# A gated recurrence and a four-branch merge: second layers taken two blocks at a time in the order H, L, D, w1 reloads two beats later, attention inputs and w2 asked for earlier

One Trainium2 chip, one core. The metric is the device time of one execution in microseconds (us), the median of several runs; less is better.

## The reference

```python
# attention: a recurrence per (batch, head), 4 x 8 x 768 x 48
for t in range(S):
    state = alpha[:, :, t, :, None] * state + np.einsum('bhd,bhe->bhde', k[:, :, t], v[:, :, t])
    y[:, :, t] = np.einsum('bhd,bhde->bhe', q[:, :, t], state)
# x = y as (3072, 384); then four branches, w1[e] 384 x 1024, w2[e] 1024 x 384
p = domain_probs / (domain_probs.sum(-1, keepdims=True) + 1e-09)
for e in range(E):
    h = np.maximum(x @ w1[e], 0.0)
    out += p[:, e:e + 1] * (h @ w2[e])
```

## The kernel before

The 24 blocks of 128 rows are worked in seven groups of 2, 4, 4, 4, 4, 4 and 2. For each group and branch, `up` computes the hidden layer in eight chunks of 128 features and `down` the second layer for each block. The attention of the next group runs in small steps between these matmuls (`advance`).

A number is split in three parts: `top` (H below), `low` (L) and `dif` (D). In the profile of before a block's split second layer takes 24 matmuls of 0.174 us, 4.2 us, a raw one 5.3 us; that it takes three parts to be exact enough is the kernel's premise. A product then takes three matmuls: L and H parts are summed in one PSUM tile, D parts in another. The first two groups still use raw weights in places, split them and store the split tiles in a "kept" copy in HBM; later groups load the copy. The four middle groups use split weights in both layers: 16 second layers of 4 x 24 matmuls.

```python
    def split_piece(l, i):                       # a raw w1 or w2 tile becomes a split one
        ...                                      # ACT, yield, ACT, yield, then
        nc.vector.scalar_tensor_tensor(out=low, ...)
        nc.vector.tensor_sub(dif, low.bitcast(F32), top.bitcast(F32))
        nc.gpsimd.dma_start(out=kept[l][i % (E * NQ)], in_=w.bitcast(F32))
        if l == 0 and i + NQ < E * NQ:
            del wt[0][i]
            load_piece(0, i + NQ)                # raw w1 of the next branch, on the sync queue

    def hidden_parts(x, parts):                  # end of a chunk of up
        top, low, dif = parts
        nc.scalar.activation(out=top, in_=x, func=ACT.Relu, scale=TRIM)      # H
        yield
        nc.vector.scalar_tensor_tensor(out=low, in0=x, ...)                  # L
        make_dif(*(part[:, :n // 2] for part in parts))                      # D, first two blocks
        later.append([part[:, n // 2:] for part in parts])                   # D, others, in down

    def down(gi, e, slot):                       # one block
        ...
        sums = [ps.tile([P, DM], F32, name=f"ops{j}", tag="g", bufs=4) for j in range(2 ...)]
        kinds = (1, 0), (2,)                     # (L, H) for each chunk, then D for each chunk
        for n, (kind, fc) in enumerate(...):
            ...
            for part in kind:
                nc.tensor.matmul(sums[part // 2], lhsT=h[:, part], rhs=w[:, part], ...)
        ...                                      # acc += p * sum, on the DVE, for both sums
```

In the profile of the kernel before, L567 is this last matmul, L520 makes H, L522 L and L530 D; L497 adds the two sums of the first layer; L480 and L488 are matmuls of `up`; L203 and L204 ask for raw w1, L206 for raw w2, L160 for alpha, k and q, L222 stores a kept tile; L580 adds a sum to the output. The changed kernel has the same lines under other numbers, given where they are shown.

In the views, PE is TensorE (PEld its weight loads, PEclk its granted clock in tenths), DVE is VectorE, ACT ScalarE, POOL GpSimd, and SPq the sync engine's DMA queue. A line of a waits view gives who waited, for what, and then the us in total, the number of waits and the longest. A line of a timeline gives start and duration in us, and in brackets the idle time before it and what ended that.

## Time and profile before

| | before |
|---|---|
| median of 4 runs | 1132.24 us (1131.76 to 1134.52) |
| span of the profiled run | 1132.4 us |
| TensorE busy | 1076.6 us |
| half-clock time of TensorE | 27 us in six stretches |
| DMA | 273.68 MB, mean 242 GB/s |

TensorE is the bound (busy for 1076.6 of 1132.4 us); what can be won is its idle time and the stretches in which its clock is at half. The prediction below shows the lines that tell who causes the idle time.

### The profile page before, as it was taken

The numbers are of one execution on the slowest core, as the hardware profiler recorded it, in microseconds if no ns is written. First come the engines' busy times: TensorE is split into PE (matmuls) and PEld (weight loads), VectorE is DVE, ScalarE is ACT, GpSimd is POOL, SyncE is SP. The second block draws the span as 40 slices with busy tenths as digits, with TensorE's granted clock in tenths as the row PEclk, the third lists the DMA queues.
The fourth block names the chain that finished last, engine by engine and source line by source line (L and its number), as shares of the span: only waits on it lengthen the run. The fifth ranks groups of instructions, "written<-read, shape, count | busy, mean of one in ns | idle before, by whom it ended". The sixth has DMA issues, their size and how long they took to land.

```text
span 1132.4 us, 21704 instructions
## 1 busy us (share of the span) xinstructions
PE 1076.6 (95%) x8532; PEld 896.4 (79%) x8532; DVE 751.5 (66%) x1625; ACT 561.2 (50%) x1191; POOL 35.5 (3%) x75
## 2 busy tenths in 40 slices
PE   8968898899999999999999999999999999999898
PEld 8746675676767798888898988898988888888676
DVE  4557776466566878777987776987776867656111
ACT  5747665565557545435546435555445344322221
POOL 2000000000000100000000000000000000000000
PEclk9989999999999999999999999999999999999999
DMA  8376869786777968548668559567569557743882
GB/s 122 108 253 190 276 212 330 282 278 241 282 236 239 364 215 337 228 149 342 217 195 339 202 178 346 183 232 304 205 210 347 203 207 290 308 183 160 296 304 74
DMA packets 166197, 273.68 MB, mean 242 GB/s; under 512 B 120624, under 2 KB 140976, under 8 KB 142032
## 3 DMA queue, kind: packets, MB, share of 16 engines
q1 hardware_dynamic: 156704, 230.06, 59.0%
q0 software_dynamic: 6016, 42.08, 9.3%
q8 instruction: 67, 1.10, 0.4%
q10 hardware_dynamic: 3376, 0.17, 0.3%
q14 instruction: 34, 0.28, 0.1%
HBM read 229.81 MB, written 42.47 MB: 240 GB/s over the span
## 4 chain that ended last, share of the span: by engine, by line
PE 72%; DVE 12%; ACT 7%; DMA 4%; issue 3%; SPq 2%; ACTq 0%; DVEq 0%
PE ops L567 21%; PE one L488 16%; PE ops L565 13%; PE two L488 7%; PE sc L324 4%; PE yps L411 4%; DVE hT L522 3%; DVE t L497 3%; PE one L480 3%; PE tp L259 3%; ACT hT L520 2%; ACT qb L298 2%; DMA ra<-in_alpha_dram 2%; DVE near L334 2%; DMA hT<-in_moe_w_dram 2%
## 5 line engine op out<-in xcount | busy, mean ns | idle before, releaser
L567 PE MATMUL ops<-w,hT 128*128 128x384 f32 x1536 | 289.3, 342 | 15.6 <-DVE hT L522 15.3
L567 PEld LDWEIGHTS ops<-w,hT 128*128 128x128 f32 x1536 | 266.7, 189 | 23.5 <-DVE hT L522 20.1
L488 PE MATMUL one<-xT,w 128*128 128x512 f32 (+1 forms) x1104 | 275.4, 385 | 0.1
L488 PEld LDWEIGHTS one<-xT,w 128*128 128x128 f32 x1104 | 194.7, 188 | 42.8 <-issue 3.2
L565 PE MATMUL ops<-hT 128*128 128x384 f32 x512 | 181.0, 500 | 10.3 <-DMA hT<-in_moe_w_dram 10.3
L495 ACT ACTIVATE t<-one 128x512 f32<-128x512 f32 (+1 forms) x184 | 102.9, 559 | 147.1 <-PE one L488 146.5
L298 ACT COPY qb<-QT 64x256 f32<-64x256 f32 x336 | 136.5, 406 | 67.9 <-DVE QT L279 38.5
L565 PEld LDWEIGHTS ops<-hT 128*128 128x128 f32 x512 | 94.9, 194 | 69.3 <-DMA hT<-in_moe_w_dram 7.5
L488 PE MATMUL two<-xT,w 128*128 128x512 f32 (+1 forms) x552 | 148.5, 377 | 0.0
L520 ACT ACTIVATE hT<-t 128x512 fp32r<-128x512 f32 x128 | 80.9, 632 | 99.9 <-DVE t L497 98.7
L522 DVE SCALAR_TENSOR_TENSOR hT<-t,hT 128x512 fp32r<-128x512 f32 x128 | 88.7, 693 | 61.2 <-ACT hT L520 59.8
L488 PEld LDWEIGHTS two<-xT,w 128*128 128x128 f32 x552 | 100.3, 188 | 19.8
L580 DVE SCALAR_TENSOR_TENSOR acc<-ops,p_all,acc 128x384 f32<-128x384 f32 x88 | 54.3, 617 | 83.9 <-PE ops L565 48.6
L530 DVE SCALAR_TENSOR_TENSOR hT<-hT 128x256 fp32r<-128x256 f32 x256 | 101.6, 423 | 4.4
L497 DVE TENSOR_TENSOR t<-t,two 128x512 f32<-128x512 f32 x128 | 87.3, 682 | 20.1 <-PE two L488 12.0
L334 DVE COPY_PREDICATED near<-masks,sc 128x256 f32<-128x256 uint8 x144 | 77.0, 535 | 25.0 <-PE sc L324 22.2
L305 DVE TENSOR_TENSOR QT<-QT,dec 128x256 f32<-128x256 f32 x144 | 60.7, 422 | 43.1 <-ACT qb L298 42.6
L324 PEld LDWEIGHTS sc<-qb,KT 128*64 128x64 f32 x2304 | 72.5, 138 | 9.4 <-issue 6.9
L500 DVE TENSOR_TENSOR hT<-t,two 128x512 f32<-128x512 f32 (+1 forms) x56 | 32.1, 574 | 70.6 <-ACT t L495 61.9
L324 PE MATMUL sc<-qb,KT 128*64 128x64 f32 x2304 | 76.7, 223 | 0.3 <-ACT qb L298 0.3
L317 DVE TENSOR_TENSOR KT<-KT,dec 128x256 f32<-128x256 f32 x144 | 60.4, 420 | 3.3 <-PE tp L259 3.3
L316 ACT COPY KT<-KT 128x256 f32<-128x256 f32 x144 | 59.7, 415 | 3.1
(79 smaller groups left out, 936.5 us busy)
## 6 DMA issues: line engine op xcount, KB each, us to landing
w<-kept SPq DMA_DIRECT2D x156, 1152.0 KB
kept<-w POOLq DMA_DIRECT2D x32, 1152.0 KB, 7.3
hT<-in_moe_w_dram SPq DMA_DIRECT2D x48, 384.0 KB
w<-in_moe_w_dram SPq DMA_DIRECT2D x60, 128.0 KB
ra<-in_alpha_dram SPq DMA_DIRECT2D x23, 192.0 KB
rk<-in_k_dram SPq DMA_DIRECT2D x23, 192.0 KB
rq<-in_q_dram SPq DMA_DIRECT2D x23, 192.0 KB
out_dram<-acc POOLq DMA_DIRECT2D x22, 192.0 KB, 2.9
```

Of the source, the lines that this page charges most:

```text
L298: nc.scalar.copy(out=qb[rows, :, i, :].rearrange("p a (b r) -> p a b r", r=m), in_=qv[rows])
L305: nc.vector.tensor_mul(qv, qv, spread(dv[:, :, :, 0], m))
L324: nc.tensor.matmul(out[HALF * s:HALF * (s + 1), 2 * p:2 * p + 2, :], lhsT=KTs[li][:, p, HALF * s:HALF * (s + 1)], rhs=qbs[li][:, p, :, QUA ...
L334: nc.vector.copy_predicated(near.rearrange("p a (b two r) -> p a b two r", two=2, r=m)[:, :, :, 1, :], mk.unsqueeze(1).broadcast_to([P, H, ...
L488: nc.tensor.matmul(out, lhsT=w[:, part, kc], rhs=xTs[gi][:, part, kc, :n], start=(part == terms[0] and kc == 0), stop=(part == terms[-1] a ...
L495: nc.scalar.activation(out=t, in_=one, func=ACT.Copy, scale=FINE)
L497: nc.vector.tensor_add(t, t, two)
L520: nc.scalar.activation(out=top, in_=x, func=ACT.Relu, scale=TRIM)
L522: nc.vector.scalar_tensor_tensor(out=low, in0=x, scalar=0.0, in1=top.bitcast(F32), op0=ALU.max, op1=ALU.subtract)
L530: nc.vector.scalar_tensor_tensor(out=dif, in0=top.bitcast(F32), scalar=1 / 4096.0, in1=low.bitcast(F32), op0=ALU.mult, op1=ALU.subtract)
L565: nc.tensor.matmul(sums[0], lhsT=h[:, 2].bitcast(F32), rhs=w, **ends)
L567: nc.tensor.matmul(sums[part // 2], lhsT=h[:, part], rhs=w[:, part], start=(fc == 0 and part != 0), stop=(fc == FCH - 1 and part != 1))
```

## The change

Its intent: fewer stalls of TensorE. (1) `down` takes two blocks of a split layer at a time, first all H products of both, then all L, then all D, so that L and D of the last chunk are wanted later. (2) alpha, k and q of a next block are asked for as soon as each buffer has been read. (3) The reload of a raw w1 tile waits two more beats of the background work, so that it doesn't stand ahead of those inputs in the sync queue. (4) Raw w2 is asked for earlier in the second and the last group. (5) The splits of the next x are spread over the last branch. (The new `down` also makes the D parts and takes the attention and background steps at other matmuls; with (3), up to four tiles may be split at once, not three.)

```diff
@@ split_piece, background
         if l == 0 and i + NQ < E * NQ:
+            for _ in range(2):
+                yield
             del wt[0][i]
             load_piece(0, i + NQ)
-        if making and len(splitting) < 3:
+        if making and len(splitting) < 4:
@@ attention
         nc.scalar.copy(out=AT, in_=turned(pair(ra)))
+        after = u + 2 if u == 0 else u + 1 if u > 1 else len(units)
+        load(after, "a")
         ...
+        load(after, "k")
         ...
         nc.vector.tensor_mul(QT, turned(pair(rq)), AT)
-        load(u + 2 if u == 0 else u + 1 if u > 1 else len(units), "akq")
+        load(after, "q")
@@ up
-        if fc in ((0,) if gi == 0 else (2, 4)) and begins and not split2(gi, e):
-            half = range(NQ) if gi == 0 else range(fc - 2, fc)
+        if fc in ((0, 2) if gi == 1 else (0,)) and begins and not split2(gi, e):
+            half = range(fc, fc + 2) if gi == 1 else range(NQ)
@@ down (cut)
-    def down(gi, e, slot):
+    def down(gi, e, slots, between):
+        sums = [[ps.tile([P, DM], F32, name=f"ops{j}", tag="g", bufs=4)
+                 for j in range(2 if halves_ else 1)] for _ in slots]
+        steps = [(part, i, fc) for part in ((0, 1, 2) if halves_ else (3,))
+                 for i in range(len(slots)) for fc in range(FCH)]
+        for n, (part, i, fc) in enumerate(steps):
             ...
+            if part >= 2 and fc == FCH - 1:
+                add_up(gi, e, slots[i], sums[i])
```

More of the change, by code (lines that the diff above doesn't have):

```diff
@@ L535, in rectified @@
         yield
-    def down(gi, e, slot):
-        cb, b = groups[gi][slot]
+    def down(gi, e, slots, between):
         first = (gi * E + e) * NQ
-        if slot == 0 and makes[1](gi, e):
+        halves_ = split2(gi, e)
+        if slots[0] == 0 and makes[1](gi, e):
             making.extend(split_piece(1, first + k) for k in range(NQ))
-        if makes[0](gi, e) and 0 < e < E - 1 and slot == 0:
+        if slots[0] == 0 and makes[0](gi, e) and 0 < e < E - 1:
             making.extend(split_piece(0, first + k) for k in range(2, NQ))
-        cols = slice(slot * P, (slot + 1) * P)
-        sums = [ps.tile([P, DM], F32, name=f"ops{j}", tag="g", bufs=4)
-                for j in range(2 if split2(gi, e) else 1)]
-        kinds = (1, 0), (2,)
-        for n, (kind, fc) in enumerate((kind, fc) for kind in (kinds if split2(gi, e) else ((),))
-                                       for fc in range(FCH)):
-            c, f = divmod(fc, FPQ)
-            h = hidden[c][:, :, f, cols]
-            ends = dict(start=(fc == 0), stop=(fc == FCH - 1))
-            if split2(gi, e):
-                w = wt[1][first + c].rearrange("p t (c d) -> p t c d", d=DM)[:, :, f]
+        sums = [[ps.tile([P, DM], F32, name=f"ops{j}", tag="g", bufs=4)
[3 more added lines that the diff above has]
+        for n, (part, i, fc) in enumerate(steps):
+            c, f = divmod(fc, FPQ)
+            h = hidden[c][:, :, f, slots[i] * P:(slots[i] + 1) * P]
+            advance(cost(1, gi, e) / FCH / (3 if halves_ else 1))
+            while between and n >= between[0][0] * len(steps):
+                between.popleft()[1]()
+            if n == len(steps) // 2:
+                background()
+            if later and n % 5 == 4:
+                make_dif(*later.popleft())
+            if halves_:
+                w = wt[1][first + c].rearrange("p t (c d) -> p t c d", d=DM)[:, part, f]
+                nc.tensor.matmul(sums[i][part // 2], lhsT=h[:, part], rhs=w,
+                                 start=(fc == 0 and part != 1), stop=(fc == FCH - 1 and part != 0))
@@ L556, in down @@
             else:
                 w = wt[1][first + c].rearrange("p (c d) -> p c d", d=DM)[:, f]
-            if n:
-                advance(cost(1, gi, e) / FCH * (len(kind) / 3 if split2(gi, e) else 1))
-            if n == FCH // 2:
-                background()
-            if later and n % 4 == 3:
-                make_dif(*later.popleft())
-            if not kind:
-                nc.tensor.matmul(sums[0], lhsT=h[:, 2].bitcast(F32), rhs=w, **ends)
-            for part in kind:
-                nc.tensor.matmul(sums[part // 2], lhsT=h[:, part], rhs=w[:, part],
-                                 start=(fc == 0 and part != 0), stop=(fc == FCH - 1 and part != 1))
@@ L569, in down @@
-        while later and slot == len(groups[gi]) // 2 - 1:
-            make_dif(*later.popleft())
+                nc.tensor.matmul(sums[i][0], lhsT=h[:, 2].bitcast(F32), rhs=w,
+                                 start=(fc == 0), stop=(fc == FCH - 1))
+            if part >= 2 and fc == FCH - 1:
+                add_up(gi, e, slots[i], sums[i])
+        background()
+        if slots[-1] == len(groups[gi]) - 1:
+            while makes[1](gi, e) and (making or splitting):
+                background()
+            for c in range(NQ):
+                del wt[1][first + c]
+                if c < NQ // 2:
+                    load_piece(1, first + NQ + c)
+                else:
+                    late.append(first + NQ + c)
@@ L571, in down, with add_up @@
+    def add_up(gi, e, slot, sums):
+        cb, b = groups[gi][slot]
         at = b * NCB + cb
@@ L586, in down @@
                 out=out[row:row + P, :], in_=acc))
-        background()
-        while slot == len(groups[gi]) - 1 and makes[1](gi, e) and (making or splitting):
-            background()
-        if slot == len(groups[gi]) - 1:
-            for c in range(NQ):
-                del wt[1][first + c]
-                if c < NQ // 2:
-                    load_piece(1, first + NQ + c)
-                else:
-                    late.append(first + NQ + c)
     def cost(layer, gi, e):
@@ L684 @@
             advance(cost(0, 0, 0) / 2)
-        down(0, 0, 0)
+        down(0, 0, [0], deque())
         while waiting:
@@ L696 @@
                 advance(cost(0, gi, e) / (2 if rest else 1))
-            if e == E - 1 and gi + 1 < len(groups):
-                behind = {0: [0], 1: [1, 2]} if len(groups[gi]) == 2 else {1: [0], 2: [1], 3: [2]}
-            else:
-                behind = {}
-            for slot in range(rest, len(groups[gi])):
-                if slot in behind:
-                    split_x(gi + 1, behind[slot])
-                down(gi, e, slot)
-                advance(cost(1, gi, e) / FCH * (2 / 3 if split2(gi, e) else 1))
+            each = 2 if split2(gi, e) else 1
+            turns = [range(k, k + each) for k in range(rest, len(groups[gi]), each)]
+            for k, slots in enumerate(turns):
+                between = deque()
+                if e == E - 1 and gi + 1 < len(groups):
+                    for kc in range(KC):
+                        at = (kc + 1) / (KC + 1) * len(turns) - k
+                        if 0 <= at < 1:
+                            between.append((at, lambda kc=kc: split_x(gi + 1, [kc])))
+                down(gi, e, slots, between)
                 if gi == len(groups) - 1 and e == E - 1:
```

## The prediction

> **What bounds the kernel now.** I read the page's first two parts first (who is busy, slice by slice), then TensorE's own waits, then the timeline around the longest of them.
>
> ```profile
> PE 1076.6 (95%) x8532; PEld 896.4 (79%) x8532; DVE 751.5 (66%) x1625; ACT 561.2 (50%) x1191; POOL 35.5 (3%) x75
> PEclk9989999999999999999999999999999999999999
> ```
>
> TensorE is busy for 1076.6 of 1132.4 us. The change removes no matmul, so all it can touch is the other 56 us and the few slices where the clock is not full. Who causes the idle time is told by the view of TensorE's waits:
>
> ```profile
> PE ops L567 <- DVE hT L522: 15.3, 13, 1.8
> PE ops L565 <- DMA hT<-in_moe_w_dram: 10.3, 5, 3.4
> PE tp L259 <- DMA ra<-in_alpha_dram: 9.9, 2, 9.7
> PE yps L411 <- ACT lat L396: 6.6, 5, 2.9
> PE far L379 <- ACT qb L298: 4.3, 5, 1.3
> PE one L480 <- DMA w<-in_moe_w_dram: 1.7, 1, 1.7
> ```
>
> L567 is the second layer of the four middle groups (split weights, 16 layers of 96 matmuls), L565 that of the outer groups (raw weights). The change aims at the first three lines: 35.5 us. The first is thirteen small stalls, one at the start of nearly every split second layer; the third is one stall of 9.7 us. The timeline of the sync engine's queue shows the cause of that one, and TensorE's timeline what it costs:
>
> ```profile
> 57.88 6.96 SPq L203 DMA_DIRECT2D w<-in_moe_w_dram  x2
> 64.89 2.56 SPq L204 DMA_DIRECT2D w<-in_moe_w_dram  x1
> 67.55 1.31 SPq L160 DMA_DIRECT2D ra<-in_alpha_dram  x1
> ...
> 75.07 1.09 PE L259 MATMUL tp<-ident,ra 128*128 128x128 f32 x4 [9.71 <-DMA ra<-in_alpha_dram]
> 75.95 2.77 PE L480 MATMUL one<-xT,w 128*128 128x256 f32 x6
> ```
>
> The next block's alpha is asked for at 67.55 only, because a raw w1 reload ahead of it sits in the same queue from 57.88 to 67.45. TensorE wants alpha at 65.4.
>
> The timeline of the start of one split second layer, all engines:
>
> ```profile
> 951.33 2.59 PE L567 MATMUL ops<-w,hT 128*128 128x384 f32 x14
> 951.84 0.58 ACT L495 ACTIVATE t<-one 128x512 f32<-128x512 f32 x1
> 951.96 0.69 DVE L522 SCALAR_TENSOR_TENSOR hT<-t,hT 128x512 fp32r<-128x512 f32 x1 [0.70 <-ACT hT L520]
> 952.69 0.42 DVE L530 SCALAR_TENSOR_TENSOR hT<-hT 128x256 fp32r<-128x256 f32 x1
> 953.03 0.68 DVE L497 TENSOR_TENSOR t<-t,two 128x512 f32<-128x512 f32 x1
> 953.75 0.63 ACT L520 ACTIVATE hT<-t 128x512 fp32r<-128x512 f32 x1 [1.33 <-DVE t L497]
> 954.41 0.69 DVE L522 SCALAR_TENSOR_TENSOR hT<-t,hT 128x512 fp32r<-128x512 f32 x1 [0.70 <-ACT hT L520]
> 955.16 2.01 PE L567 MATMUL ops<-w,hT 128*128 128x384 f32 x10 [1.23 <-DVE hT L522]
> ```
>
> TensorE runs 14 matmuls (L and H of hidden chunks 0 to 6, in pairs) at 0.174 us each and stops at the L part of chunk 7. That chunk's H is ready at 954.38 (end of L520), its L at 955.10 (end of the last L522).
>
> [...]
> - [...] nothing of L567 starts between matmul 14's want and 955.16.
> - [...] six L480 matmuls took 2.77 us after the 9.7 us stall and 1.46 us elsewhere, and the granted clock of 70 to 75 us was 0.50.
> - [...]
>
> **The change, part by part.**
>
> (1) Order H, L, D over two blocks. It removes no work. It moves the first use of chunk 7: before, its L at matmul 14; after, its H at matmul 7, as H of the first block runs through all eight chunks before the second block begins. In the layer shown: matmul 7 is reached at 951.33 + 7 x 0.174 = 952.55, H is there at 954.38, so a stall of 1.9 us. It then reaches matmul 14 at 954.43 + 7 x 0.174 = 955.65, where before it was 955.16: 0.5 us later, not sooner. Nothing in the diff shortens the chain that makes H of chunk 7 (copy 0.58, the DVE's L and half D of chunk 6 at 0.69 and 0.42, add 0.68, H 0.63). I read the same four times in all 16 layers: the stall after the change (H of chunk 7, less when matmul 7 is reached) is 1.5 to 3.0 us in twelve, 0.2 to 0.7 in four, sum 26 us. Before, the same layers lost 17 us (the view says 15.3, as it counts a matmul's modelled tail as busy). **About +9.5 us.**
>
> (2) All four PSUM tiles in one pair. Before, a block's two sums had 24 matmuls (4.2 us and more) until a later block needed their banks. After, the next pair's first matmul needs the first block's sum only eight matmuls (1.4 us) after that block's last. The DVE adds take 0.62 us each. I measured, for each block, how long after its last matmul starts the add of its first sum ends: in nine of 16 layers the second block's is under about 1 us, so no stall; in five it is 1.4 to 2.4; in the last layers of two groups (near 532 and 704 us), where the DVE has the next x to split, it is 4.9 us. With both blocks' adds together at the end, the first block's first sum comes some 1.35 us before the second's. In those two layers that leaves a stall of 2.5 us each; in the five about 0.4. **About +7 us.**
>
> (3) Attention inputs asked for once used, w1 reloads two beats later. The 9.7 us stall can go: alpha is asked for near 51 us, where the DMA engines are nearly idle (share 0.22 from 50 to 55 us), and the reload no longer stands ahead of it. But from 55 to 65 us they are at 0.94, mostly with the kept-weight stores, and the same bytes have still to come. In the kernel before, the third and fourth raw w1 tiles of the next layer are asked for at 74.2 and 76.3 and are just in time only because TensorE has lost 9.7 us. Without that loss it wants them about 69 and 73 us, and the last now stands behind the raw w2. So I take 4 of the 9.7 back as a new wait for raw w1, about 4 us. Less half-clock time afterwards (2.77 to 1.46 and smaller ones) is within this. **About -6 us**, between -1 and -12.
>
> (4) Raw w2 asked for earlier. In the second group at the first and third instead of third and fifth chunk: 3.0 us of stall at 211 us goes, with 1 us of half clock (0.69 granted from 210 to 215). In the last group all at once: 1.6 and 2.0 us at 1056 and 1061 us go, with 1 us of clock. The 3.4 us stall at 176 us is in the first group, whose request isn't moved. **About -8.5 us**, if the DMA engines, at 0.95 to 1.05 there, deliver w2 first.
>
> (5) Next x spread: the same three splits at the same places for the four-block groups. **0.**
>
> Sum: +9.5 + 7 - 6 - 8.5 = +2 us on 1132.
>
> **Rivals.**
> (A) The early stretch is cured fully and the order costs little: if TensorE's stall in (1) gives the DVE time to catch up, the adds of (2) come in time. Then +9.5 - 12 - 10 = -12: 1120. For it: the DVE is idle in the stall. Against: in the two worst layers the DVE timeline has no gap over 0.1 us from 536 to 555 us.
> (B) The intent holds: H first means that TensorE waits for less, and the 15.3 us go as well: about 1105. For it: in layers where H of chunk 7 is early (1.5 us after the start in two of them) nearly nothing is lost. Against: in twelve of 16 it is later than 2.9 us.
> (C) The wait only changes name early on: raw w1 or w2 land as late as alpha did, gain (3) is nothing, and (2) is worse, 12 us: 1145. For it: DMA at 0.94; against: the idle DMA before 55 us is now used.
>
> **Range and chances.** The sum is 1134; since the person who made the order chose it for some reason that I may not see, I shade it towards (A) and say **1131 us**. Extremes of (A) and (C) with a little more give 1116 to 1145. Faster by over 2% needs under 1109.5, which only (B) gives: 0.05. Slower by over 2% needs 1154.8, beyond (C): 0.03. Within 2%: 0.92.
>
> **What would show it right or wrong.** Right: the waits of L567 name ACT's H part (L520's successor) instead of DVE's L, over 20 us in all, and some for the DVE's adds near 543 and 715 us; the 9.7 us wait for alpha is gone with a few us for raw w1 between 60 and 80 us; no wait for w2 at 211 and 1056 us. Wrong: L567's waits for H under 12 us (then (1) fails), no waits for adds (then (2) fails), or the first 110 us shortened by 10 us or by nothing (then (3) is mis-sized).

Where the prediction says banks, it means the PSUM tiles of the code's rotation (`bufs=4`).

## The result

| | before | after |
|---|---|---|
| median of 4 runs | 1132.24 us | 1147.02 us (1145.63 to 1147.94) |
| ratio, 95% interval | | 1.0125 (1.0108 to 1.0143) |
| span of the profiled run | 1132.4 us | 1146.2 us |
| half-clock time of TensorE | 27 us | 38 us |

A ratio is the mean time of one kernel's fast runs over that of the other's fast runs of the same rounds, so it is not quite the ratio of the medians. The change made the kernel 1.25% slower: within 2%, as predicted, but 2 us beyond the predicted range and on the side that the sum of the steps pointed to.

The first two parts of the page of the changed kernel, and its TensorE waits:

```profile
PE 1080.6 (94%) x8532; PEld 900.0 (79%) x8532; DVE 752.4 (66%) x1625; ACT 562.7 (49%) x1191; POOL 35.5 (3%) x75
PEclk9989898999999999999999999999999999999999
```

```profile
PE one L485 <- DMA w<-in_moe_w_dram: 23.6, 10, 9.1
PE ops L568 <- ACT hT L525: 23.2, 15, 2.1
PE yps L416 <- ACT lat L401: 4.9, 4, 3.5
PE ops L568 <- DVE acc L599: 3.6, 2, 1.9
```

(Here L485 is the raw first layer, L568 the split second layer, L525 makes H and L599 adds a sum.) All three waits that the change aimed at are gone: none for L, for alpha or for raw w2. Three others are there in their place: for H instead of L (23.2 against 15.3), for the adds (3.6), and for raw w1 (23.6, where it was 1.7).

Lining up the starts of the same layers in both traces gives a ledger of where the changed kernel falls behind:

| stretch | lag gained by the changed kernel | predicted |
|---|---|---|
| start to the first split second layer (402.5 us of before) | +5.1 us | -10 |
| 402.5 to 1045.9 us (middle groups) | +14.2 us | +16.5 |
| 1045.9 us to the end | -5.6 us | -4.5 |

So the middle and the end came within 2.3 us of what was predicted, and the early stretch did not. Inside it the lag is +14.4 us when the fourth branch's second layer begins (171.3 us of before), after which the missing w2 waits win most of it back. By the waits of that stretch in both traces, raw w1 costs 21.9 us more, alpha 9.9 less, raw w2 6.7 less and the attention steps 3.4 less; 6.8 us more at half clock cost up to 3.4: +5.3 in all.

The timeline of the changed kernel at the start of the same layer that the prediction showed (there at 951.33, here at 969.66; L500 is the copy, L527 makes L, L502 the add; lines of other work are left out):

```profile
969.66 1.38 PE L568 MATMUL ops<-w,hT 128*128 128x384 f32 x7
970.17 0.58 ACT L500 ACTIVATE t<-one 128x512 f32<-128x512 f32 x1
970.30 0.69 DVE L527 SCALAR_TENSOR_TENSOR hT<-t,hT 128x512 fp32r<-128x512 f32 x1 [0.70 <-ACT hT L525]
971.36 0.68 DVE L502 TENSOR_TENSOR t<-t,two 128x512 f32<-128x512 f32 x1
972.08 0.63 ACT L525 ACTIVATE hT<-t 128x512 fp32r<-128x512 f32 x1 [1.33 <-DVE t L502]
972.76 2.00 PE L568 MATMUL ops<-w,hT 128*128 128x384 f32 x10 [1.71 <-ACT hT L525]
```

Seven matmuls, then a stop until H of the last chunk is there: 3.10 us after the start. Before, it was fourteen, and a stop until L was there, 3.83 us after the start. The chain on ACT and DVE takes the same time in both (2.54 us from the start of the copy to the end of H).

The sync queue around the longest new stall. First the last raw w1 tile of the fourth branch in the kernel before (columns: start, duration; the tile ahead of it was asked for at 151.9), then raw w2 and the last two raw w1 tiles in the changed kernel, with what TensorE made of it:

```profile
156.45 1.33 SPq L203 DMA_DIRECT2D w<-in_moe_w_dram  x2
157.83 0.60 SPq L204 DMA_DIRECT2D w<-in_moe_w_dram  x1
```

```profile
160.40 3.37 SPq L206 DMA_DIRECT2D hT<-in_moe_w_dram  x4
163.87 1.38 SPq L203 DMA_DIRECT2D w<-in_moe_w_dram  x2
165.31 0.78 SPq L204 DMA_DIRECT2D w<-in_moe_w_dram  x1
166.19 9.29 SPq L203 DMA_DIRECT2D w<-in_moe_w_dram  x2
175.53 2.02 SPq L204 DMA_DIRECT2D w<-in_moe_w_dram  x1
...
178.02 1.22 PE L485 MATMUL one<-xT,w 128*128 128x256 f32 x2 [9.13 <-DMA w<-in_moe_w_dram]
```

Before, both tiles were asked for ahead of raw w2 (which followed at 158.5). Now they stand behind it, and issuing the last takes from 166.2 to 177.6 us: the kept stores of this branch have begun at 160, and the DMA share of 170 to 175 us is 1.02.

The second longest is in the second branch, where the 9.7 us stall for alpha had been:

```profile
62.33 0.70 PE L485 MATMUL one<-xT,w 128*128 128x256 f32 x2 [1.67 <-DMA w<-in_moe_w_dram]
69.27 2.07 PE L485 MATMUL one<-xT,w 128*128 128x256 f32 x4 [6.24 <-DMA w<-in_moe_w_dram]
```

This is the branch's first raw w1 tile. It was asked for at 51.4 us before, and at 54.8 here, behind alpha and k; the DMA share of the next ten microseconds is 1.05 and 1.01.

### The profile page after: what moved, and what is told of

Same layout as the page of the kernel before. It is cut to its first block, busy times and chain, and to the rows that moved or that the text cites. A ratio compares the mean times of both kernels' runs of the same rounds, so it can differ in the third digit from the quotient of the medians.

```text
span 1146.2 us, 21704 instructions
## 1 busy us (share of the span) xinstructions
PE 1080.6 (94%) x8532; PEld 900.0 (79%) x8532; DVE 752.4 (66%) x1625; ACT 562.7 (49%) x1191; POOL 35.5 (3%) x75
## 4 chain that ended last, share of the span: by engine, by line
PE 75%; DVE 12%; ACT 6%; DMA 4%; issue 2%; SPq 1%; POOL 0%; DVEq 0%; ACTq 0%; POOLq 0%
PE ops L568 22%; PE one L493 16%; PE ops L572 13%; PE two L493 7%; PE sc L329 4%; PE yps L416 4%; DMA w<-in_moe_w_dram 4%; DVE t L502 3%; DVE hT L527 3%; PE tp L261 3%; PE one L485 3%; ACT hT L525 3%; DVE near L339 2%; ACT qb L303 1%; PE sps L437 1%
## 5 line engine op out<-in xcount | busy, mean ns | idle before, releaser
L568 PE MATMUL ops<-w,hT 128*128 128x384 f32 x1536 | 293.8, 345 | 26.9 <-ACT hT L525 23.2
L568 PEld LDWEIGHTS ops<-w,hT 128*128 128x128 f32 x1536 | 269.9, 191 | 35.7 <-ACT hT L525 28.5
L493 PEld LDWEIGHTS one<-xT,w 128*128 128x128 f32 x1104 | 195.0, 188 | 41.4 <-issue 3.2
L500 ACT ACTIVATE t<-one 128x512 f32<-128x512 f32 (+1 forms) x184 | 103.1, 560 | 164.2 <-PE one L493 163.7
L572 PE MATMUL ops<-hT 128*128 128x384 f32 x512 | 176.2, 491 | 0.0
L527 DVE SCALAR_TENSOR_TENSOR hT<-t,hT 128x512 fp32r<-128x512 f32 x128 | 88.7, 693 | 61.0 <-ACT hT L525 59.6
L525 ACT ACTIVATE hT<-t 128x512 fp32r<-128x512 f32 x128 | 80.9, 632 | 97.1 <-DVE t L502 95.9
L599 DVE SCALAR_TENSOR_TENSOR acc<-ops,p_all,acc 128x384 f32<-128x384 f32 x88 | 54.3, 617 | 93.2 <-PE ops L572 43.4
L502 DVE TENSOR_TENSOR t<-t,two 128x512 f32<-128x512 f32 x128 | 87.3, 682 | 20.8 <-PE two L493 12.7
L485 PE MATMUL one<-xT,w 128*128 128x256 f32 (+1 forms) x240 | 55.1, 371 | 24.4 <-DMA w<-in_moe_w_dram 23.6
L485 PEld LDWEIGHTS one<-xT,w 128*128 128x128 f32 x240 | 39.6, 205 | 35.3 <-DMA w<-in_moe_w_dram 30.4
```

Of the source, the lines that this page charges most:

```text
L485: nc.tensor.matmul(one, lhsT=w[:, kc], rhs=xraws[gi][:, kc, lo:hi], start=(kc == 0), stop=(kc == KC - 1))
L493: nc.tensor.matmul(out, lhsT=w[:, part, kc], rhs=xTs[gi][:, part, kc, :n], start=(part == terms[0] and kc == 0), stop=(part == terms[-1] a ...
L500: nc.scalar.activation(out=t, in_=one, func=ACT.Copy, scale=FINE)
L502: nc.vector.tensor_add(t, t, two)
L527: nc.vector.scalar_tensor_tensor(out=low, in0=x, scalar=0.0, in1=top.bitcast(F32), op0=ALU.max, op1=ALU.subtract)
L568: nc.tensor.matmul(sums[i][part // 2], lhsT=h[:, part], rhs=w, start=(fc == 0 and part != 1), stop=(fc == FCH - 1 and part != 0))
```

## The experiments

Twelve kernels. "L" below stands for the later reload (with the limit of four tiles that comes with it), "A" for the inputs asked for once used, "W" for the earlier w2, "O" for the new second layer with the spread of x; so the changed kernel is before + L + A + W + O. Runs of one call share the runs of the kernel before, whose median moved between 1129.4 and 1132.9 us from call to call; ratios are the safer figures.

| run | what it is | median us | ratio to before (95%) |
|---|---|---|---|
| m_late | A W O | 1140.14 | 1.0084 (1.0053 to 1.0116) |
| p_late | L | 1131.73 | 1.0010 (0.9980 to 1.0041) |
| m_order | L A W | 1127.77 | 0.9977 (0.9951 to 1.0003) |
| p_order | O | 1149.20 | 1.0181 (1.0143 to 1.0220) |
| p_w2 | W | 1122.01 | 0.9936 (0.9918 to 0.9953) |
| p_attn | A | 1127.38 | 0.9980 (0.9956 to 1.0004) |
| q7 | last chunk last, one block | 1117.79 | 0.9895 (0.9875 to 0.9915) |
| o7 | O with last chunk last | 1131.95 | 1.0020 (0.9993 to 1.0047) |
| q7_w | q7 + W | 1111.21 | 0.9804 (0.9772 to 0.9836) |
| q7_aw | q7 + A W | 1107.77 | 0.9779 (0.9752 to 0.9805) |
| q7_law | q7 + L A W | 1115.45 | 0.9845 (0.9819 to 0.9872) |
| thin | changed kernel, stores a third | 1130.49 (1 run) | not compared |

### The order, undone and alone

m_order is the changed kernel with the old `down`; p_order is the kernel before with the new one. The edits are the last hunk of the diff, taken out or put in alone.

> The changed kernel with the old second layer (one block at a time, L and H in pairs, then D), all else kept. Theory T2 (the order costs what the ledger between 402 and 1046 us shows): 1131 to 1135 us, waits for H gone, waits for L of 14 to 16 us back, no wait for the adds. Rival: the middle lost its 14 us to something else (input requests moved in the queue, weights later), then over 1141 us.

> The kernel before with the new second layer alone (two blocks at a time, H, L, D, with the spread of next x that comes with it). T2: 1144 to 1148 us, with 22 to 25 us of waits for H and 3 to 5 us for the adds. Rival: as the early stretch is untouched, a time within 4 us of before if the middle's loss came from the input requests.

TensorE's waits in p_order:

```profile
PE ops L563 <- ACT hT L520: 23.2, 15, 2.1
PE ops L563 <- DVE acc L594: 3.7, 2, 1.9
```

m_order's longest waits:

```profile
PE one L485 <- DMA w<-in_moe_w_dram: 19.9, 11, 5.5
PE ops L572 <- DVE hT L527: 15.2, 13, 1.8
```

p_order is 1.8% slower than before, and its trace loses 14.2 us in the middle stretch, as the changed kernel does; m_order loses nothing there (it gains 2) and runs at 1127.8, slightly under its expected 1131 to 1135. p_order's 1149.2 is 1 us over its expected range. Both show the waits that were expected. **The order costs the middle groups some 14 us; this holds alone and with the rest.** By the ratios the order costs more, 1.8% alone and 1.5% with the rest (20 and 17 us); what lies beyond the middle has no cause shown. (The traces of before and p_order differ by 13.3 us only, but that of before is one of its slow executions, 1134.2 us, and that of p_order its fastest.) That it isn't the moved input requests is shown by p_order, which has none of them. m_order shows one thing more, for the early stretch: without the new order the waits for raw w1 are still 19.9 us, and by 402.5 us of before it has won 0.5 us and not the 10 predicted.

### When the last chunk is wanted

If the cause is only when chunk 7 of the hidden layer is wanted, then any order that wants it later must win. q7 changes the old `down` for the first block of a layer only:

```diff
+        steps = [(kind, fc) for kind in kinds for fc in range(FCH)]
+        if split2(gi, e) and slot == 0:
+            steps = [s for s in steps if s[1] < FCH - 1] + [s for s in steps if s[1] == FCH - 1]
```

o7 does the like within the two-block order, in a layer's first pair: L and H of chunk 7 of both blocks come after L and H of the other seven. All else is as in p_order, so the two differ by the order alone.

> The kernel before with one change of mine: in the first block of a split second layer, the three products of the last hidden chunk come after all others (L and H of chunks 0 to 6, then D of 0 to 6, then chunk 7), so chunk 7 is wanted at the 22nd matmul (3.7 us after the start) and not at the 15th (2.4 us). Theory (the start of the layer waits for the chain that makes chunk 7, and it is only a matter of when it is wanted): waits for L fall from 15.3 to under 4 us, time 11 to 15 us under before. Rival: TensorE then waits for the D parts or the adds, as the DVE is behind; time within 5 us of before.

> The kernel before with the new second layer (two blocks, H, L, D), but in its first pair H and L of the last hidden chunk of both blocks come after H and L of chunks 0 to 6 (wanted at the 29th matmul). Theory: the 23.2 us of waits for H go to under 3 us, so 18 to 23 us under the run with the new second layer alone, 1126 to 1131 us; the waits for the adds stay at 3 us or grow to 10, as TensorE comes sooner to the end of the pair while the DVE doesn't. Rival: the two-block order costs for another reason, then over 1140 us.

TensorE's waits in the split second layer, q7 first, then o7:

```profile
PE ops L569 <- DVE hT L522: 2.4, 5, 0.6
PE ops L569 <- DVE hT L530: 1.0, 2, 0.5
```

```profile
PE ops L567 <- DVE acc L598: 10.7, 6, 3.8
PE ops L567 <- ACT hT L520: 0.7, 1, 0.7
```

q7 brings the waits for L from 15.3 to 2.4 us and the time down by 1.05%, some 12 us. o7 brings the waits for H from 23.2 to 0.7 us: the two-block order loses them for the same reason. But o7 is no faster than before and 1 us over its expected range, as **the waits for the adds then grow from 3.7 to 10.7 us** (my bound was 10). TensorE comes earlier to the end of a pair, while the DVE doesn't, and both blocks' sums fill all four PSUM tiles. In the kernel before, with one block at a time, the view of TensorE's waits has no wait for the adds. So the two-block order has two costs: it wants H of the last chunk too early, and it leaves no spare PSUM tile (read from the code and these waits; no run had more tiles). The first hides a part of the second.

### The early stretch: one part at a time

> The kernel before with the earlier requests for raw w2 alone. Theory: the waits for raw w2 fall from 10.3 us to under 4 us (the one at 176 us is in the first group and stays), time 6 to 9 us under before. Rival: with the DMA engines at their limit there, w2 comes earlier at the cost of the first layer's weights, then waits for w1 or kept weights grow as much and the time is within 2 us of before.

p_w2 is 0.64% faster (7.2 us by the ratio), within what was expected, and loses no time elsewhere: the raw w2 waits fall from 10.3 to 3.3 us, those for raw w1 stay at 1.8 (1.7 before).

> The kernel before with attention inputs asked for once used, alone (reloads as before). Theory T (the alpha wait is mostly passed on to raw w1, because alpha, k, q and the reloads of this stretch share DMA engines that the kept-weight stores fill from 55 to 68 us): alpha plus w1 waits between 9 and 15 us where before had 11.6, time within 3 us of before. Rival: queue order alone made the alpha wait; then alpha plus w1 waits under 5 us and the time 7 to 11 us under before.

```profile
PE one L483 <- DMA w<-in_moe_w_dram: 5.9, 4, 4.1
PE ops L568 <- DMA hT<-in_moe_w_dram: 5.2, 6, 1.9
...
PE tp L259 <- DMA ra<-in_alpha_dram: 3.2, 1, 3.2
```

In p_attn alpha plus w1 come to 9.1 us (11.6 before), the low end of theory T, and the gain of 0.2% is not clear of noise. Of the 6.7 us that the alpha wait lost, 4.2 came back as waits for raw w1, even with the reloads at their old place.

### The later reload

m_late is the changed kernel with the two extra beats and the limit of four taken out; p_late is before with them put in.

> The changed kernel with the later w1 reloads taken out (no two extra beats, at most three tiles in the making), all else of the change kept. Theory T (the later reload, behind raw w2 and attention inputs in the sync queue, makes the 23.6 us of waits for raw w1): those waits fall under 8 us, the alpha wait of 9.7 us stays away or is under 4 us, and the time is 1128 to 1137 us. Rival R (the DMA engines are full, so the alpha wait was passed on to w1 and would be with any order of the queue): waits for w1 and alpha together stay over 15 us and the time is 1142 to 1147 us.

> The kernel before with the later w1 reloads alone. T: waits for raw w1 appear (8 to 20 us), as the last two tiles of each layer still come behind raw w2; the alpha wait shrinks, as the reload no longer stands ahead of it; time 1132 to 1145 us. R: the sum of the alpha and w1 waits stays near the 11.6 us of before, time 1130 to 1135 us.

The waits of m_late up to 200 us:

```profile
PE one L483 <- DMA w<-in_moe_w_dram: 10.9, 3, 4.6
...
PE tp L259 <- DMA ra<-in_alpha_dram: 3.5, 1, 3.5
```

Neither side of the expectation was met by m_late: w1 plus alpha wait 14.4 us (T said w1 under 8, R said the sum over 15), and the time, 1140.1, lies between. The later reload thus makes some 9 of the 23.6 us, not all. What it costs the changed kernel in time is not shown by this pair: 1.0125 and 1.0084, and their intervals overlap. In p_late the w1 waits come to 15.4 us and alpha's shrink to 1.8; a sum of 17.2 against 11.6, as T said. Yet p_late costs nothing clear in time (1131.7, within R's range and just under T's): by 334 us its layers lag by 0.6 us, and its waits for raw w2 are 4.1 us in all against 10.3 before. A later pair shows the cost plainly: q7_law against q7_aw, which differ by the later reload alone.

> The same with the later w1 reloads too, so the whole change but its order of the second layer, with mine in its place. If the later reload costs by itself: 3 to 7 us over the run without it (1108 to 1116 us), with waits for raw w1 of 15 to 22 us. Rival: the later reload is harmless without the two-block order: within 2 us of the run without it.

```profile
PE one L485 <- DMA w<-in_moe_w_dram: 20.8, 9, 6.1
```

> The same with attention inputs asked for once used (reloads as before). If that adds its own -2 to -7 us: 1103 to 1110 us. Rival: the alpha wait passed on to w1, 1110 to 1114 us.

```profile
PE one L483 <- DMA w<-in_moe_w_dram: 6.2, 3, 4.2
...
PE tp L259 <- DMA ra<-in_alpha_dram: 3.6, 1, 3.6
```

With it 1115.45, without it 1107.77 us on the same chip: 7.7 us, a little over the 3 to 7 expected. The rival, that it is harmless without the two-block order, falls for this setting; p_late, without A and W, showed no cost.

### Why the wait is passed on: the kept stores

The remaining question is whether the queue's order makes these waits or the DMA engines are full. thin leaves the order of the queue as in the changed kernel and takes away two thirds of the bytes stored for w1:

```diff
-        nc.gpsimd.dma_start(out=kept[l][i % (E * NQ)], in_=w.bitcast(F32))
+        nc.gpsimd.dma_start(out=kept[0][i % (E * NQ)][:, 0], in_=w[:, 0].bitcast(F32))   # l == 0
```

> The changed kernel, but of each split w1 tile only the first third is stored to the kept copy (and read back three times), so the result is wrong on purpose and only the stretch up to 185 us is judged: the stores there are 0.38 MB instead of 1.15 MB each, the order of the queue is the same. Theory T (the early waits are the DMA engines filled by the kept stores, whatever the order): the waits for raw w1 up to 185 us fall from 23.6 to under 8 us. Rival Q (the order of the sync queue alone: w1 behind inputs and raw w2): they stay over 15 us.

```profile
PE one L492 <- DMA w<-in_moe_w_dram: 5.6, 9, 1.3
```

The waits for raw w1 fall from 23.6 to 5.6 us, with the longest at 1.3, and the second group begins 18 us sooner than in the changed kernel. (The result was wrong; with the top part in place of all three it still passed the comparison's tolerance. Only the stretch up to 185 us is used.) So the stores are needed for these waits: **the same queue order costs 23.6 us of waits with the whole stores and 5.6 us with a third of their bytes.** With the whole stores the order matters too, as m_late shows: with the reloads at their old place the waits for raw w1 are 10.9 us and not 23.6, but alpha's are 3.5 and not 0. In p_attn, where alpha moved ahead, w1 waits 4.2 us longer and alpha 6.7 us less. What neither thin nor m_late gives alone is a split of the 23.6 us into two fixed shares; the two act together.

### The version that beats both

> My order of the first block plus the earlier requests for raw w2, nothing else of the change. If the two gains add: -11.7 and -7.4 us by their own runs, so 1109 to 1113 us. Rival: the gain of w2 in the last group shrinks, as that group starts with the same DMA load but TensorE elsewhere is faster: 1113 to 1117 us.

q7_w and q7_aw put my order of the first block together with the parts that pay. q7_w runs at 1111.2 us; the gains of W and of q7 add (0.9936 x 0.9895 = 0.983, measured 0.980). q7_aw is the best: **1107.8 us, 2.2% under before (95%: 1.95 to 2.48%) and some 3.4% under the changed kernel** (by their ratios 0.9779 and 1.0125). Its expectation of 1103 to 1110 us held.

## Why the prediction was wrong

By its own steps:

- **Step (1), the order: right.** Predicted: waits for H over 20 us in all and +9.5 us. Measured: 23.2 us of waits for H in the changed kernel and in p_order, 7.9 more than the 15.3 for L before. That the moment of the want decides these waits was shown by q7 and o7.
- **Step (2), PSUM tiles: right in kind, too large.** +7 us predicted, 3.6 us of waits measured, both of them in the two layers named (at 554 and 731 us). The 2.5 us for each of these two doesn't follow from the figures given for it (4.9 less 1.35 is 3.5); 1.85 and 1.75 were measured. The five layers that were to lose 0.4 us each lost nothing. That TensorE's stall for H lets the DVE catch up fits o7, where without that stall the waits for the adds come to 10.7 us.
- A term that the sum lacked: half-clock stretches. Three of 3.4 us fall in the middle groups of the changed kernel, one in the kernel before; at half speed two more cost up to 3.4 us (in the kernel before six matmuls of the raw first layer took 2.77 us at a granted clock of 0.50 and 1.46 us at 1.00). It makes up for what step (2) was too large by: 7.9 + 3.6 + 3.4 is 14.9, and the middle came out at 14.2 against 16.5.
- **Step (4), w2: right.** All waits for it are gone, and W alone gives 7.2 us against 8.5.
- **Step (3), the step that failed.** It said "I take 4 of the 9.7 back as a new wait for raw w1, about 4 us" and "About -6 us", between -1 and -12. The waits for raw w1 grew by 21.9 us, from 1.7 to 23.6. The cause was named (DMA share 0.94 from 55 to 65 us, mostly stores; the last tile stands behind w2), but it was applied to the third and fourth tile of one branch only. In that branch, where the 9.7 us stall had been, the waits came to 11.6 us and not 4: 7.9 of them for the first tile, which had moved behind alpha and k and into the stores, 3.6 for the third and fourth. Another 12.0 us, which the sum lacked altogether, are in the two later branches (2.7 us at 126 us, 9.3 at 178 us), where there had been no alpha wait to win back. The prediction's own sign for a mis-sized step (3) came: the first 93 us were not shortened, but 1.8 us longer. With the early stretch at +5.1 instead of -10 us the error there is 15 us, more than the 13 between the sum of +2 and the 14.8 measured. Of these 15, 9.5 are there without the new order (m_order: -0.5 instead of -10). The other 5.6 come only with it; see the open point below.
- The shading from 1134 to 1131 towards rival (A), for reasons outside the profile, went the wrong way. Of the rivals, (C) was the nearest: the wait changed its name, for the reason given there. Its counter-argument, idle DMA before 55 us, was true (share 0.22 from 50 to 55 us in the kernel before; in the changed kernel there is no wait for alpha) and did not help, since w1 was then behind.

One small slip: rival (B), with 15.3 + 6 + 8.5 us won, comes to 1102 and not 1105 us; nothing rests on it.

One thing stays open. With L, A and W in place, the old order lags by 4.7 us at the start of the second group and the new one by 9.8 (alone, in p_order, by 3.0), though the new `down` does the same matmuls in the same order there. It only shifts when attention steps and background beats fall. Which shift makes the last tile later (9.1 us of wait at 178 us, against 4.8 and 2.2 in m_order) was not tested.

## What to carry to other kernels

When a stall waits for the last link of a chain, work out when each order first needs that link: here an order had shorter waits where it put more work ahead of the first need (15.3 us of waits with it at the 15th matmul in the kernel before, 23.2 at the 8th in the changed kernel, 2.4 at the 22nd in q7), whatever it did for later needs. When a request is moved ahead in a queue, look at what is now behind it: here 4.2 of the 6.7 us that alpha's wait lost came back as waits for raw w1 (p_attn). Look for all places where the same load recurs, not only where the stall stood. And count the buffers that a wider step takes: two blocks at once used all four tiles, and the waits for the adds went from none to 3.6 us, and to 10.7 us in o7.

## What else the traces show

- Stalls and half clock, in the middle groups. In the changed kernel stalls of 2.0 to 2.1 us (496.4 to 498.6, 673.6 to 675.7 and 1046.1 to 1048.1 us) were each followed within 0.7 us by 3.41 us at half clock, while one of 2.00 us that ended at 892 us and those of 1.4 to 1.85 us were not. In the kernel before one of 1.83 us, which ended at 1029.8 us, was followed by such a stretch 1.3 us later. What decides it is not shown.
- The two queues while both are in use. From 55 to 65 us of the kernel before, the store queue sent 377 packets with 3.1 MB and the sync queue 1547 packets with 0.41 MB (54% of them of 128 bytes or less): about four packets for each of the other's, and about an eighth of the bytes.
- From 170 to 175 us, within its longest stall, the changed kernel moved 402 GB/s, loads and stores together, at a DMA share of 1.02.
